# A new order of all steps, four half sums moved from VectorE to accumulating DMAs, and two copies moved to ScalarE

## The chip, the cores and the metric

The kernel runs on one core of a Trainium2 chip. A core has a TensorE for matmuls (PE; its weight loads are listed as PEld), a VectorE (DVE), a ScalarE (ACT), a GpSimd (POOL) and a SyncE (SP), and 16 DMA engines that move data between the chip's memory and the on-chip memory. The engines run side by side; each executes its own instructions in the order in which they were written, and semaphores make one wait for another. The metric is the device time of one execution in microseconds (us). Lower is better.

## The reference

The reference is a gated linear attention followed by a feed-forward layer with a rational activation. For each of 4 batches and 8 heads of 48 columns, over 768 positions:

```python
f = 1.0 / (1.0 + np.exp(-f_logit))
for t in range(S):
    state = f[:, :, t, :, None] * state + np.einsum('bhd,bhe->bhde', k[:, :, t], v[:, :, t])
    y[:, :, t] = np.einsum('bhd,bhde->bhe', q[:, :, t], state)
```

The result, reordered to 3072 rows of 384, goes through the layer:

```python
h = x @ w_in                      # 384 -> 2048
P = a[0] + a[1] * h + a[2] * h2 + a[3] * h3
Q = 1.0 + np.abs(b[0]) * np.abs(h) + np.abs(b[1]) * h2
g = P / (Q + 1e-06)
return g @ w_out                  # 2048 -> 384
```

Inputs and output are float32; the kernel computes in bfloat16 with float32 accumulation.

## The kernel before

The work is cut into 12 units of 256 positions: three stretches of time for each of four batches. A unit is an attention part, which hands its state to the next unit of the same batch, and a feed-forward part on 2048 hidden columns, which stand as 16 blocks of 128. There is no loop that sets the order. A text named ORDER lists 824 steps, one after another; the code walks through it and records each step's instructions. A step's name is followed by its unit, then by the heads' range or by the first and last block it covers (`0 8` is the first half of the 16, `8 16` the second, `0 16` all). `@0` to `@3` names one of four places in PSUM that the step's result takes, and `>x` makes the step begin only behind the step x. Every engine, and every DMA queue, executes its steps in the order in which they stand in this text.

The steps of a unit's attention part are these. `ld` loads gates, keys, queries (from SP's queue) and values (from POOL's queue, which also converts them). `ef` and `ls` turn the gates into logarithms on ACT. `cs` sums them over time on PE, and `A` takes the exponential of plus and minus these sums on ACT. `xa` multiplies queries and keys by that on DVE, `xg` does the same on POOL. `T` transposes both on PE, and `Te` copies the transposes out of PSUM (on ACT if an `s` follows, else on DVE). `sc` forms scores on PE, `mk` masks them on DVE. `vm` copies slices of the values on POOL. `yb` and `yi` form the output from scores and from the old state, `ye` scales it into the feed-forward layer's input (`s` on ACT, `v` on DVE). `kv` and `si` form the new state, `ae` and `st` decay it. `cm`, `cz`, `cu`, `ci`, `fa`, `fb` and `fr` prepare constants, and `dz` runs matmuls whose result nobody reads.

The feed-forward part is: `h`, 12 matmuls for four blocks of hidden columns; `hy`, the copy of these to bfloat16 (on ACT, or on DVE if a `v` follows); `sq` (h2, the square) and `ab` (z, the absolute value) on DVE. Then the logarithm of Q is taken on ACT. Its argument is the sum z + h2, which is made in one of three ways: by matmuls with the identity (`u`, then `ln` on ACT), by a DVE add (`zv`, then `lz`), or by a DMA that adds h2 onto z in memory (`zd`, then `lz`). `ex` on ACT turns this into 1/Q. The numerator is built on DVE: `p1` (a[3]h + a[2]), `pm` (times h2), `p2` (a[1]h + a[0], written over h), then the sum of the two, either by a DVE add (`tv`) or by a DMA that adds (`ta`); `gm` multiplies by 1/Q. Last come `o` (the second matmul, four blocks for one of two halves of the positions), `oe` (copy out of PSUM) and `so` (store).

The accumulating DMAs `zd` and `ta` are issued by POOL, between its `vm` copies, `xg` products and loads. Three buffers each hold h and the numerator over successive units, two hold h2 and z. In the lines that follow a number behind an underscore tells such buffers apart; it differs between the two kernels.

Of the kernel before, what the change touches and what calls it, by code (L numbers as in the profile page):

```python
# [24 lines left out]
ld 1 v; yb 0 2 4 @2; mk 0 0; wi 4 8; st 0 0; A 1 1; wi 0 4; yb 0 0 2; xa 1 1; yi 0 1; si 0 1; dz 3 @0; A 1 0
xa 1 0; dz 3; st 0 1; ye 0 0 1 v; ye 0 1 3 s; T 1 @1; Te 1 s; vm 1 1; fb; vm 1 0; ld 2 v; h 0 8 12 @2
hy 0 8 12 v; vm 2 1; sc 1 0 @0; ef 2; sc 1 1 @3; vm 2 0; mk 1 1; ha 0 12 16 @1; hb 0 12 16; ld 3 f >ye.0.0.1
ls 2; kv 1 @2; si 1 0; dz 1 @3; cs 2 @3; hy 0 12 16; ae 1; mk 1 0; ld 2 k; yb 1 2 4 @0; ab 0 8 12; ld 3 v
yb 1 0 2; st 1 0; A 2 1; yi 1 1; si 1 1; ld 4 v; sq 0 8 12; A 2 0; h 0 4 8 @1; ye 1 s; ef 3; h 1 12 16 @3
hy 0 4 8; ls 3; sq 0 12 16; p1 0 8 16; ab 0 12 16; st 1 1; hy 1 12 16; h 1 8 12 @0; hy 1 8 12; h 0 0 4 @2  # L30
pm 0 8 16; p2 0 8 16; cs 3 @3; ld 2 q; ab 0 4 8; sq 0 4 8; hy 0 0 4; ld 3 k; ld 3 q; u 0 12 16 @1; xa 2 1
sq 1 8 16; A 3 1; xa 2 0; sq 0 0 4; ln 0 12 16; ld 4 f; h 1 4 8 @2; A 3 0; hy 1 4 8; T 2 @0; u 0 8 12 @3
p1 0 0 8; ab 0 0 4; ab 1 8 16; Te 2 s; h 1 0 4 @1; ln 0 8 12; p2 0 0 8; sc 2 0 @2; xa 3 0; xg 3 1 0 2 >xa.3.0
hy 1 0 4; kv 2 @0; sc 2 1 @3; mk 2 0; u 1 12 16 @2; si 2 0; xg 3 1 2 4 >mk.2.0; ex 0 8 16; mk 2 1; p1 1 0 16
# [73 lines left out]
def kernel(  # L108
# [161 lines left out]
    def ef(n, a0=0, a1=HP):  # L270
        f = unit(n)["f"][:, 2 * a0:2 * a1].rearrange("p h i d -> p (h i d)")
        nc.scalar.activation(f, f, AF.Exp, scale=-1.0)  # L272
# [255 lines left out]
    def zd(n, m0, m1):  # L528
        s = unit(n)
        nc.gpsimd.dma_start(out=fl(s["z"], m0, m1), in_=fl(s["h2"], m0, m1), accum_op=ALU.add)  # L530
# [106 lines left out]
```

## Time and profile before

| what | value |
|---|---|
| time, median of 3 runs | 215.97 us (213.47 to 216.31) |
| span of the profiled execution, first to last instruction | 212.2 us |
| time of that profiled execution itself | not given with the results |
| accumulating DMAs, `gall<-hy` (`ta`) and `z<-h` (`zd`) | 18 and 15 |
| bytes moved by DMA, mean rate over the span | 41.10 MB, 194 GB/s |

In the profile an instruction is named by the line of the code, its engine, its operation and its tiles. A group of equal instructions has a count, the busy time in us, the mean duration of one in ns, and the time that the engine stood idle ahead of them with what ended it. `L564` is the DVE add `tv`, `L526` the DVE add `zv`, `L560` and `L530` are the DMAs `ta` and `zd`, `L495` is `hy`, `L338` and `L336` are `Te` on DVE and on ACT, `L441` and `L442` are `ye` on DVE and on ACT, `L534` is `lz`, `L460` is `h`, `L578` is `o`. A busy engine can still be the one that nobody waits for, so the stages and the waits are read beside the shares.

### The profile page before, as it was taken

To read this page: it belongs to the slowest core of one execution; us is meant where nothing else is said; L and a number is where in the kernel's file an instruction comes from. 1 tells how busy PE (TensorE), PEld (TensorE's weight loads), DVE (VectorE), ACT (ScalarE), POOL (GpSimd) and SP (SyncE) were. 2 spreads that over 40 slices of the span, in tenths; PEclk is the share of its full clock that TensorE was granted. 3 is DMA by queue.
4 is the path that set the end of the run, shared out by engine and by line. 5 is a ranking of instruction groups with operands and counts; after the bars stand their busy time and mean duration, and the time that the engine had idled before them with its cause. 6 is when DMAs were issued, how large, how long until landed. Compare 5 with 4: busy or idle time off the path is not lost.

```text
span 212.2 us, 7141 instructions
## 1 busy us (share of the span) xinstructions
PE 202.0 (95%) x3167; PEld 140.4 (66%) x3167; DVE 200.3 (94%) x210; ACT 193.2 (91%) x195; POOL 86.5 (41%) x106
## 2 busy tenths in 40 slices
PE   4999999989999999999999999999999989999993
PEld 1466677557776675677686686686686667676551
DVE  4786989999999999999999999999999999999991
ACT  3565699999999999899999999999999999999990
POOL 6151222661324793633136447397356143133100
PEclk9999999999999999999999999999999999999999
DMA  5999999999899999999299999599997996949924
GB/s 138 244 200 215 233 241 223 255 235 214 152 187 74 237 207 240 259 197 213 73 237 238 238 235 182 97 191 244 201 189 150 186 173 117 198 89 274 204 116 153
DMA packets 60623, 41.10 MB, mean 194 GB/s; under 512 B 51120, under 2 KB 54960, under 8 KB 60592
## 3 DMA queue, kind: packets, MB, share of 16 engines
q0 software_dynamic: 20944, 21.76, 63.5%
q1 hardware_dynamic: 39360, 18.68, 34.1%
q8 instruction: 25, 0.41, 0.8%
q10 hardware_dynamic: 288, 0.20, 0.3%
q14 instruction: 6, 0.05, 0.1%
HBM read 25.17 MB, written 4.72 MB: 141 GB/s over the span
## 4 chain that ended last, share of the span: by engine, by line
PE 18%; ACT 16%; DVE 14%; issue 5%; DMA 4%; ACTq 0%; POOLq 0%
PE op L578 12%; PE hp L460 5%; ACT hy L495 4%; ACT qi L538 4%; DMA z<-h 4%; ACT lq L534 3%; DVE h L500 3%; DVE scm L359 2%; DVE gall L568 2%; ACT qkT L336 1%; DVE gall L542 1%; ACT A L303 1%; DVE z L508 1%; DVE gall L556 1%; DVE gall L564 1%
## 5 line engine op out<-in xcount | busy, mean ns | idle before, releaser
L578 PE MATMUL op<-w_out_sb,gall 128*128 128x384 bf16 x384 | 69.0, 326 | 0.0
L460 PE MATMUL hp<-xT,w_in_sb 128*128 128x256 bf16 x564 | 67.6, 273 | 1.4 <-ACT xT L442 0.7
L460 PEld LDWEIGHTS <-w_in_sb 128*128 128x128 bf16 x564 | 54.3, 98 | 11.2 <-issue 1.5
L578 PEld LDWEIGHTS <-gall 128*128 128x128 bf16 x384 | 36.2, 98 | 22.7 <-DVE gall L568 0.5
L495 ACT CAST hy<-hp 128x1024 bf16<-128x1024 f32 x47 | 49.3, 1090 | 1.1 <-PE hp L489 1.0
L538 ACT ACTIVATE qi<-lq 128x4096 bf16<-128x4096 f32 (+2 forms) x18 | 45.6, 2539 | 0.0
L534 ACT ACTIVATE lq<-z 128x2048 f32<-128x2048 bf16 (+1 forms) x20 | 36.8, 1878 | 0.3 <-DMA z<-h 0.3
L560 POOL DMA_DIRECT2D gall<-hy x18 | 19.3, 1124 | 28.4 <-DVE gall L556 10.8
L359 DVE TENSOR_TENSOR scm<-sc,mask 128x1024 bf16<-128x1024 f32 x24 | 28.8, 1217 | 0.6 <-PE sc L351 0.6
L314 POOL TENSOR_TENSOR qkp<-kn,A 128x384 bf16<-128x384 f32 x17 | 17.0, 1002 | 29.8 <-ACT alast L447 7.4
L500 DVE TENSOR_TENSOR h<-hy 128x4096 bf16<-128x4096 bf16 (+2 forms) x19 | 28.3, 1500 | 0.2 <-ACT hy L495 0.2
L568 DVE TENSOR_TENSOR gall<-gall,qi 128x4096 bf16<-128x4096 bf16 (+2 forms) x17 | 28.2, 1668 | 0.2
L366 POOL COPY vmp<-vn 128x128 bf16<-128x128 bf16 x24 | 20.3, 919 | 19.7 <-DMA vn<-in_v_dram 18.4
L556 DVE TENSOR_TENSOR gall<-gall,h 128x4096 bf16<-128x4096 bf16 (+2 forms) x17 | 28.2, 1665 | 0.0
L530 POOL DMA_DIRECT2D z<-h x15 | 14.9, 1051 | 24.9 <-DVE h L500 7.2
L303 ACT ACTIVATE A<-cs 128x768 f32<-128x768 f32 (+1 forms) x26 | 19.7, 800 | 3.7 <-PE cs L287 2.9
L547 DVE TENSOR_SCALAR hy<-hy,a_sb 128x4096 bf16<-128x4096 bf16 (+1 forms) x14 | 16.7, 1192 | 0.0
L542 DVE TENSOR_SCALAR gall<-hy,a_sb 128x4096 bf16<-128x4096 bf16 (+1 forms) x14 | 16.6, 1187 | 0.0
L508 DVE TENSOR_SCALAR z<-hy 128x4096 uint16<-128x4096 uint16 (+2 forms) x19 | 16.1, 853 | 0.0
L272 ACT ACTIVATE fn<-fn 128x768 f32<-128x768 f32 (+1 forms) x13 | 10.8, 831 | 5.4 <-DMA fn<-in_f_logit_dram 5.4
L194 POOL DMA_DIRECT2D vn<-in_v_dram x12 | 12.9, 1079 | 6.8 <-issue 6.8
L326 PE MATMUL tp<-ident,qkp 128*128 128x128 bf16 x192 | 12.8, 219 | 0.2
(74 smaller groups left out, 266.7 us busy)
## 6 DMA issues: line engine op xcount, KB each, us to landing
gall<-hy POOLq DMA_DIRECT2D x16, 512.0 KB, 7.0
z<-h POOLq DMA_DIRECT2D x13, 512.0 KB, 7.8
fn<-in_f_logit_dram SPq DMA_DIRECT2D x11, 384.0 KB, 8.4
kn<-in_k_dram SPq DMA_DIRECT2D x11, 384.0 KB, 9.4
qn<-in_q_dram SPq DMA_DIRECT2D x11, 384.0 KB, 9.7
out_dram<-osb SPq DMA_DIRECT2D x11, 384.0 KB, 3.5
vn<-in_v_dram POOLq DMA_DIRECT2D x12, 192.0 KB, 7.2
w_in_sb<-in_moe_w_in_dram POOLq DMA_DIRECT2D x4, 384.0 KB, 7.8
```

The lines of the kernel that those rows point to most:

```text
L303: nc.scalar.activation(t, src, AF.Exp, scale=1.0 if x else -1.0)
L359: return nc.vector.tensor_mul(t, s["sc", g].rearrange("s r a i t -> s (r a) (i t)"), mb)
L366: nc.gpsimd.tensor_copy(s["vm"][:, :, :, 32 * x:32 * x + 16], src)
L460: nc.tensor.matmul(t[:, m - m0, :], w_in_sb[:, kk, m * P:(m + 1) * P], s["x"][:, kk].rearrange("p i j t -> p (i j t)"), start=(kk == 0), s ...
L495: (nc.scalar.copy if eng == "s" else nc.vector.tensor_copy)(fl(big(s, "hy", "hy", 3), m0, m1), fl(s["hp", m0], 0, m1 - m0))
L500: return nc.vector.tensor_mul(fl(big(s, "h2", "h2", 2), m0, m1), fl(s["hy"], m0, m1), fl(s["hy"], m0, m1))
L534: nc.scalar.activation(fl(lq, m0, m1), fl(s["z"], m0, m1), AF.Ln, scale=regs[2], bias=1.0 + 1e-6)
L538: nc.scalar.activation(fl(qi, m0, m1), fl(lq, m0, m1), AF.Exp, scale=-1.0)
L556: return nc.vector.tensor_mul(fl(s["g"], m0, m1), fl(s["g"], m0, m1), fl(s["h2"], m0, m1))
L560: nc.gpsimd.dma_start(out=fl(s["g"], m0, m1), in_=fl(s["hy"], m0, m1), accum_op=ALU.add)
L568: return nc.vector.tensor_mul(fl(s["g"], m0, m1), fl(s["g"], m0, m1), fl(qi, m0, m1))
L578: nc.tensor.matmul(s["op", j][:, j, 0:DM], s["g"][:, m, P * j:P * j + P], w_out_sb[:, m, :], start=(s["on", j] == 1), stop=(s["on", j] == KF))
```

## The change

The text ORDER is replaced. Both have 824 steps. Most are the same step at another place in the text or in another PSUM place; these nine are different steps:

| before | after |
|---|---|
| `tv 1 8 16`, `tv 2 8 16`, `tv 4 8 16` (DVE adds) | `ta 1 8 16`, `ta 2 8 16`, `ta 4 8 16` (DMAs) |
| `zv 2 8 16` (DVE add) | `zd 2 8 16` (DMA) |
| `zv 5 8 16` on DVE, `zd 5 0 8` by DMA | `zd 5 8 16` by DMA, `zv 5 0 8` on DVE |
| `Te 0 0 2` (DVE) | `Te 0 0 2 s` (ACT) |
| `hy 0 8 12 v` (DVE) | `hy 0 8 12` (ACT) |
| `ye 3 s` (ACT) | `ye 3 v` (DVE) |

The rest of the diff makes several step functions return their instruction, so that a `>` mark can name them:

```diff
 ORDER = """
-ld 0 f 2 4; cu 1; cz 0; ab_ b a; ld 0 f 0 2; cz 2; ld 0 k 0 2; cu 0; ld 0 k 2 4; ld 0 q 2 4; ci; cm; dz 9 @0
...
+ld 0 f 0 2; cz 2; cu 0; cz 1; cz 0; ab_ b a; ld 0 f 2 4; ab_ a s; ld 0 q 2 4; ld 0 k 2 4; ld 0 k 0 2; ld 1 f
...
     def zd(n, m0, m1):
         s = unit(n)
-        nc.gpsimd.dma_start(out=fl(s["z"], m0, m1), in_=fl(s["h2"], m0, m1), accum_op=ALU.add)
+        return nc.gpsimd.dma_start(out=fl(s["z"], m0, m1), in_=fl(s["h2"], m0, m1), accum_op=ALU.add)
...
     def ta(n, m0, m1):
         s = unit(n)
-        nc.gpsimd.dma_start(out=fl(s["g"], m0, m1), in_=fl(s["hy"], m0, m1), accum_op=ALU.add)
+        return nc.gpsimd.dma_start(out=fl(s["g"], m0, m1), in_=fl(s["hy"], m0, m1), accum_op=ALU.add)
```

The same `return` is added to `ef`, `A`, `ae`, `hy`, `ln`, `lz` and `ex`.

Three places show how instructions moved. The first is DVE in the first unit, from the first transpose copy `Te 0 2 4` (`qkT<-tp`) on; `scm` is a masked score, `state` the new state, `xT` the output of `ye`. Before:

```order
L338 COPY qkT<-tp 128x4x256
L314 TENSOR_TENSOR qkp_87<-qn,A 128x2x4x48
L359 TENSOR_TENSOR scm_281<-sc,mask 128x1024
L338 COPY qkT<-tp 128x4x256
L359 TENSOR_TENSOR scm_367<-sc,mask 128x1024
L451 TENSOR_TENSOR state_1_97<-sv,alast 128x384
L314 TENSOR_TENSOR qkp_88<-kn,A 128x2x8x48
L314 TENSOR_TENSOR qkp_88<-qn,A 128x2x8x48
L451 TENSOR_TENSOR state_0_96<-sv,alast 128x384
L441 TENSOR_SCALAR xT<-y,sig 128x2x2x64
```

After:

```order
L338 COPY qkT<-tp 128x4x256
L229 TENSOR_TENSOR mask<-Ui 128x64 x2
L229 TENSOR_TENSOR mask<-Us 128x64
L229 TENSOR_TENSOR mask<-Ui 128x64
L314 TENSOR_TENSOR qkp_87<-qn,A 128x2x4x48
L359 TENSOR_TENSOR scm_293<-sc,mask 128x1024
L359 TENSOR_TENSOR scm_336<-sc,mask 128x1024
L451 TENSOR_TENSOR state_1_97<-sv,alast 128x384
L314 TENSOR_TENSOR qkp_88<-qn,A 128x2x8x48
L314 TENSOR_TENSOR qkp_88<-kn,A 128x2x8x48
L441 TENSOR_SCALAR xT<-y,sig 128x2x2x64
L451 TENSOR_TENSOR state_0_96<-sv,alast 128x384
```

The mask is built here instead of in the first microseconds, the second transpose copy has left DVE, and `ye 0` stands ahead of the second state.

The second place is ACT in the first and second unit. Before, from `ef 1` to `ae 1`:

```order
L272 ACTIVATE fn<-fn 128x768
L447 ACTIVATE alast<-sv 128x8
L277 ACTIVATE lsp_93<-fn 128x8x2x48
L303 ACTIVATE A<-cs 128x2x384 x2
L442 ACTIVATE xT<-y 128x2x4x64
L336 COPY qkT<-tp 128x1024
L272 ACTIVATE fn<-fn 128x768
L277 ACTIVATE lsp_92<-fn 128x8x2x48
L495 CAST hy_471<-hp 128x1024
L447 ACTIVATE alast<-sv 128x8
```

After, from `ls 1` to `ae 1`:

```order
L277 ACTIVATE lsp_93<-fn 128x8x2x48
L336 COPY qkT<-tp 128x4x128
L303 ACTIVATE A<-cs 128x2x384 x2
L447 ACTIVATE alast<-sv 128x8
L266 TENSOR_LOAD sig x2
L442 ACTIVATE xT<-y 128x2x4x64
L336 COPY qkT<-tp 128x1024
L272 ACTIVATE fn<-fn 128x768
L495 CAST hy_521<-hp 128x1024
L277 ACTIVATE lsp_92<-fn 128x8x2x48
L495 CAST hy_521<-hp 128x1024
L447 ACTIVATE alast<-sv 128x8
```

The half transpose copy (`qkT<-tp 128x4x128`) and the first `hy` are new on ACT; the second `ls` (`lsp_92`) stands behind that `hy`.

The third place is POOL around the sums of units 1 and 2; `vmp` is a `vm` copy, `qkp` an `xg` product, `vn` a load of values. Before:

```order
L314 TENSOR_TENSOR qkp_88<-kn,A 128x2x4x48
L194 DMA vn<-in_v_dram 128x8x96 x2
L314 TENSOR_TENSOR qkp_88<-kn,A 128x2x4x48
L560 DMA gall_1333<-hy_1144 128x2048
L366 COPY vmp_94<-vn 128x8x16
L194 DMA vn<-in_v_dram 128x8x96
L366 COPY vmp_95<-vn 128x8x16
L530 DMA z_807<-h_760 128x2048
```

After:

```order
L206 DMA w_out_sb<-in_moe_w_out_dram 128x4x384 x2
L530 DMA z_669<-h_584 128x2048
L366 COPY vmp_95<-vn 128x8x16
L194 DMA vn<-in_v_dram 128x8x96
L366 COPY vmp_94<-vn 128x8x16 x2
L560 DMA gall_1048<-hy_731 128x2048
L314 TENSOR_TENSOR qkp_88<-kn,A 128x2x4x48 x2
L366 COPY vmp_95<-vn 128x8x16
L560 DMA gall_1458<-hy_1089 128x2048
```

`z_669` is the new `zd 2 8 16`, `gall_1048` the new `ta 1 8 16`; `gall_1458` is `ta 2 0 8`, which stood first of the sums before (`gall_1333`).

More of the change, by code (lines that the diff above doesn't have):

```diff
@@ L25 @@
[L25 to L34, printed above, removed]
@@ new lines @@
+hy 0 0 4; h 1 4 8 @0; u 0 12 16 @2; A 3 0; A 3 1; hy 1 4 8; T 2 @3; ld 3 k; ld 3 q; ld 4 f; ln 0 12 16; ld 6 f
+Te 2 s; u 0 8 12 @0; ln 0 8 12; sq 1 8 16; h 1 0 4 @2; sc 2 0 @3; kv 2 @0; ld 4 k; ld 4 q; hy 1 0 4; sq 0 0 4
+vm 2 0; ex 0 8 16; p1 0 0 8; ab 1 8 16; ab 0 0 4; ab 0 4 8; ld 5 f; xa 3 0; pm 0 0 8; ld 3 v; vm 2 1; ld 5 v
+wo 8 12; wo 12 16; xg 3 1 0 2 >xa.3.0; si 2 0; sc 2 1 @1; u 1 12 16 @2; ae 2; ln 1 12 16; mk 2 0
+xg 3 1 2 4 >mk.2.0; mk 2 1; st 2 0; u 0 4 8 @3; u 0 0 4 @1; yb 2 2 4 @2; ef 4; yi 2 1; yb 2 0 2; ln 0 0 4; ye 2 s
@@ new lines @@
+ld 8 f; ld 6 q; ld 7 k; xg 5 1 2 4 >pm.2.0.16; yb 4 2 4; yb 4 0 2; cs 6 @0; o 0 0 8 12; lz 2 8 16; ye 4 s; ld 6 k
+u 2 0 4 @1; st 4 1; ab 3 0 16; sq 3 0 16; p1 3 0 16; gm 1 8 16; gm 1 0 8; A 6 0; oe 0 0 2 s; ln 2 0 4; A 6 1
+h 4 4 8 @3; T 5 @2; h 4 12 16 @1; ef 7; h 4 0 4 @0; hy 4 4 8; Te 5 s; hy 4 12 16; ex 2 8 16; hy 4 0 4; sc 5 0 @2
+h 4 8 12 @3; mk 5 0; o 1 1 8 12 @1; zv 3 8 16; u 2 4 8 @2; o 1 1 4 8; hy 4 8 12; sc 5 1 @0; kv 5 @3; p2 3 0 16
+xa 6 0; ln 2 4 8; mk 5 1; vm 5 1; ta 2 0 8; ld 6 v; ta 2 8 16; zd 3 0 8; xg 6 1 2 4 >mk.5.0; ae 5
@@ new lines @@
+xg 6 1 0 2 >gm.1.8.16; ls 7; o 1 0 8 12; o 1 0 4 8; si 5 0; o 1 1 0 4; cs 7 @2; st 5 0; ex 2 0 8; ef 8; si 5 1
+yb 5 2 4 @0; yb 5 0 2; A 7 0; sq 4 0 16; yi 5 1; yi 5 0; A 7 1; st 5 1; ld 8 q; o 1 0 12 16; ld 11 f; ld 9 k
+ld 9 q; ld 8 k; ye 5 s; o 1 1 12 16; T 6 @3; h 5 4 8 @0; lz 3 8 16; pm 3 0 16; ab 4 0 16; gm 2 0 16; Te 6 s
+o 1 0 0 4; kv 6 @2; ld 8 v; vm 6 1; zd 4 0 8; hy 5 4 8; ta 3 0 8; oe 1 0 2 s; si 6 0; xg 7 1 0 2 >gm.2.0.16
+ta 3 8 16; h 5 8 12 @3; sc 6 1 @0; h 5 0 4 @1; ls 8; ae 6; hy 5 8 12; lz 3 0 8; hy 5 0 4; o 2 1 12 16 @3
@@ new lines @@
+o 2 1 4 8; o 2 0 0 4; o 2 0 12 16; sc 6 0 @1; p1 4 0 16; st 6 0; mk 6 1; p2 4 0 16; xa 7 0; ex 3 0 16; zd 4 8 16
+vm 6 0; vm 7 1; xg 7 1 2 4 >st.6.0; mk 6 0; o 2 0 8 12; h 5 12 16 @0; si 6 1; pm 4 0 16; hy 5 12 16; o 2 0 4 8
+T 7 @1; o 2 1 0 4; lz 4 0 8; yi 6 0 @0; yi 6 1; ab 5 0 16; Te 7 s; st 6 1; yb 6 2 4; yb 6 0 2; o 2 1 8 12
+cs 8 @2; sc 7 1 @1; ye 6 s; h 6 0 4 @0; oe 2 0 2 s; A 8 1; A 8 0; hy 6 0 4; ef 11; sq 5 0 16; h 6 4 8 @3
+hy 6 4 8; mk 7 1; h 6 12 16 @2; sc 7 0 @0; kv 7 @1; p1 5 0 16; gm 3 0 16; hy 6 12 16; si 7 0; o 3 0 0 4 @3
@@ new lines @@
+so 3 0 2 s; hy 7 8 12; ld 11 q; ld 10 k; ld 10 q; Te 8; hy 7 0 4; kv 8 @2; p1 6 0 16; xa 9 0; si 8 0
+o 4 0 4 8 @1; ls 10; lz 5 0 8; ae 8; sc 8 1 @3; zd 6 8 16; sc 8 0 @0; lz 6 8 16; zd 6 0 8; vm 8 0; ta 5 0 8
+ld 10 v; o 4 0 12 16; o 4 1 0 4; o 4 0 0 4; xg 9 1 0 2 >gm.4.0.16; xg 9 1 2 4 >p1.6.0.16; mk 8 0; mk 8 1
+h 7 12 16 @0; yb 8 0 2 @3; hy 7 12 16; o 4 1 8 12; o 4 0 8 12; o 4 1 4 8; st 8 0; pm 6 0 16; yi 8 0; yi 8 1
+yb 8 2 4; p2 6 0 16; ab 7 0 16; sq 7 0 16; ex 5 0 16; kv 9 @2; si 9 0; o 4 1 12 16; cs 10 @0; ye 8 s; oe 4 0 2 s
@@ new lines @@
+o 7 0 0 4; o 7 1 4 8; hy 11 12 16; ex 9 0 16; o 8 1 0 4 @2; h 11 8 12 @3; o 8 1 4 8; o 8 0 4 8; h 11 0 4 @1
+o 8 0 0 4; o 8 0 8 12; o 8 1 8 12; sq 10 0 16; o 8 0 12 16; o 8 1 12 16; ab 10 0 16; hy 11 8 12; zv 10 0 8
+p1 10 0 16; ta 9 8 16; ta 9 0 8; ab 11 12 16; pm 10 0 16; p2 10 0 16; gm 9 0 16; lz 10 0 8; sq 11 12 16
+sq 11 8 12; p1 11 8 16; zd 10 8 16; ab 11 8 12; lz 10 8 16; o 9 1 0 4 @3; oe 7 0 2 s; so 5 0 2 s; so 6 0 2 s
+ex 10 0 16; o 9 1 8 12; o 9 1 12 16; ta 10 0 8; pm 11 8 12; o 9 0 8 12; h 11 4 8 @0; tv 10 8 16; o 9 0 12 16
@@ new lines @@
+o 9 0 0 4; o 9 1 4 8; o 9 0 4 8; p2 11 8 16; zd 11 12 16; gm 10 0 16; hy 11 0 4; hy 11 4 8; lz 11 12 16
+pm 11 12 16; sq 11 0 4; sq 11 4 8; ab 11 0 4; ab 11 4 8; p1 11 0 8; zd 11 8 12; lz 11 8 12; oe 8 0 2 s
+ex 11 8 12; oe 9 0 2 s; ex 11 12 16; ta 11 8 12; so 9 0 2 s; o 10 1 12 16 @0; o 10 0 8 12; o 10 0 12 16
+so 8 0 2 s; so 7 0 2 s; zv 11 0 4; p2 11 0 8; o 10 0 0 4; u 11 4 8 @2; o 10 1 0 4; gm 11 8 12; ta 11 12 16
+ln 11 4 8; ex 11 4 8; lz 11 0 4; o 10 1 8 12; o 10 0 4 8; o 11 1 8 12 @3; o 10 1 4 8; pm 11 4 8; gm 11 12 16
@@ L99 @@
+tv 11 4 8; ex 11 0 4; oe 10 0 2 s; gm 11 4 8; pm 11 0 4; tv 11 0 4; o 11 1 12 16; o 11 0 12 16 @1; o 11 1 4 8
+o 11 0 4 8; o 11 0 8 12; gm 11 0 4; so 10 0 2 s; o 11 0 0 4; o 11 1 0 4; oe 11 1 2 s; oe 11 0 1 v; dz 1 @1
+so 11 0 1 s; so 11 1 2 a
 """
@@ L271, in ef @@
         f = unit(n)["f"][:, 2 * a0:2 * a1].rearrange("p h i d -> p (h i d)")
-        nc.scalar.activation(f, f, AF.Exp, scale=-1.0)
+        return nc.scalar.activation(f, f, AF.Exp, scale=-1.0)
     def ls(n, a0=0, a1=HP):
@@ L494, in hy @@
         s = unit(n)
-        (nc.scalar.copy if eng == "s" else nc.vector.tensor_copy)(
+        return (nc.scalar.copy if eng == "s" else nc.vector.tensor_copy)(
             fl(big(s, "hy", "hy", 3), m0, m1), fl(s["hp", m0], 0, m1 - m0))
```

118 lines of the change are left out of this document (45 added, 73 removed).

## Prediction

> **What bounds the kernel now.** I read the page's busy line, then a table by stages, then who waits for whom, then the chain of waits from its end. The page:
>
> ```profile
> span 212.2 us, 7141 instructions
> PE 202.0 (95%) x3167; PEld 140.4 (66%) x3167; DVE 200.3 (94%) x210; ACT 193.2 (91%) x195; POOL 86.5 (41%) x106
> ```
>
> Three engines are nearly full, so the averages decide nothing. The stage table has for each stretch the busy time of PE, PEld, DVE, ACT and POOL, then clock, share of the DMA engines and GB/s:
>
> ```profile
> 0.00:27.00 27.00, 23.18 (x419) 14.53 (x420) 20.59 (x53) 14.70 (x24) 8.98 (x23) 1.00 1.14 206
> 27.00:171.00 144.00, 140.99 (x2437) 101.13 (x2434) 143.41 (x121) 142.71 (x145) 69.74 (x75) 1.00 1.04 199
> 171.00:208.60 37.60, 37.55 (x321) 24.70 (x313) 35.78 (x37) 35.81 (x29) 7.74 (x10) 1.00 0.76 173
> 208.60:212.20 3.60, 0.32 (x2) 0.00 (x0) 0.56 (x1) 0.00 (x0) 0.00 (x0) 1.00 0.32 114
> ```
>
> In the head (0 to 27) ACT idles 12.3 of 27 us and DVE 6.4. In the middle both are full at once: DVE lacks 0.6 us of 144, ACT 1.3 us. In the tail PE is full. ACT's waits for the whole span name those gaps:
>
> ```profile
> ACT fn L272 <- DMA fn<-in_f_logit_dram: 5.4, 4, 2.3
> ACT A L303 <- PE cs L287: 2.9, 3, 1.2
> ACT xT L442 <- DVE xT L441: 2.1, 1, 2.1
> ...
> ACT A L303 <- DVE qkp L314: 0.8, 1, 0.8
> ACT lq L534 <- DMA z<-h: 0.3, 1, 0.3
> ACT alast L447 <- PE sv L431: 0.2, 1, 0.2
> ```
>
> The last three are the whole 1.3 us of the middle; a DMA's sum was late once, by 0.3 us. The chain at its end runs on PE without a break:
>
> ```profile
> 171.14 1.47 PE hp L460 x12
> ...
> 191.42 8.52 PE op L578 x52
> 199.94 0.86 PE u L516 x4
> 200.80 7.83 PE op L578 x48
> ...
> 208.66 0.56 DVE osb L585
> ```
>
> **The change, part by part.** Times of a step are taken from its start to the next start, since neighbours overlap a little.
>
> Half sums off DVE. DVE loses `tv 1 8 16`, `tv 2 8 16`, `tv 4 8 16` and `zv 2 8 16`; in unit 5 it only swaps its half.
>
> ```profile
> 91.30 1.14 DVE gall L564
> ...
> 110.21 1.13 DVE z L526
> ```
>
> Four at 1.13 to 1.14 us are 4.5 us off DVE.
>
> The copies. `Te 0 0 2` and `hy 0 8 12` leave DVE for ACT, and `ye 3`, which the change's title doesn't name, comes from ACT to DVE. The DVE timeline, then ACT's:
>
> ```profile
> 11.94 0.68 DVE L338 COPY qkT<-tp 128x1024 bf16<-128x1024 bf16 x1
> ...
> 16.98 0.48 DVE L441 TENSOR_SCALAR xT<-y,sig 128x256 bf16<-128x256 f32 x1
> 17.37 0.74 DVE L260 TENSOR_SCALAR a_sb<-a_sb,sig 128x3 f32<-128x3 f32 x3
> 19.72 1.23 DVE L495 CAST hy<-hp 128x1024 bf16<-128x1024 f32 x1 [1.61 <-PE hp L460]
> ```
>
> ```profile
> 55.10 0.85 ACT L442 ACTIVATE xT<-y 128x768 bf16<-128x768 f32 x1
> 55.80 1.07 ACT L521 ACTIVATE lq<-u 128x1024 f32<-128x1024 f32 x1
> ...
> 144.16 1.99 ACT L495 CAST hy<-hp 128x1024 bf16<-128x1024 f32 x2
> 145.96 3.71 ACT L538 ACTIVATE qi<-lq 128x4096 bf16<-128x4096 f32 x1
> ```
>
> DVE: minus 0.7 and minus 1.2. `ye 3` is three times the 256 columns that took 0.39 us; my estimate is 0.9, between 0.39 and 1.17, nearer the upper end because most of the time grows with columns. DVE in all: -4.5 - 0.7 - 1.2 + 0.9 = -5.5 us. ACT: plus 0.9 for `hy 0 8 12` (two casts in 1.80 us) and about 0.5 for half a transpose copy (half of that), both in the head; minus 0.7 for `ye 3` (55.10 to 55.80), in the full middle. ACT in all: +0.7 us. So the stretch from 27 to 171 has 0.7 us less ACT work, and DVE gets some 4 us of room there that ACT can't follow.
>
> The waits in ACT's middle. The 0.8 us wait for a DVE product should go, since DVE gets ahead; the 0.3 us wait for the sum of unit 6 too, since its operands are ready earlier. I count -1.1 and leave the 0.2. What is late next there is nothing that the profile shows: ACT simply has 142 us of work. Bounds: 0 to -1.3.
>
> The head. Here the order is new on every engine. The first `sc` now waits behind `kv 0`, and the mask is built between `Te 0 2 4` and `xa 0 0 0 2`, so the first masked scores come about 1 us later; unit 1's gates are loaded one place earlier, and `ef 1` and `ls 1` move up. Both copies moved to ACT fall into its 12.3 idle us, but `ls 2`, then `cs 2` and `A 2`, stand behind `hy 0 8 12`. Against that DVE no longer has the half copy (0.7) ahead of the second masked scores, and `ye 0` overtakes `st 0 1`. Followed through step by step, `ye 1` comes out 0 to 0.5 us later, ahead of a wait of ACT that hides part of it:
>
> ```profile
> 26.83 0.84 ACT L272 ACTIVATE fn<-fn 128x768 f32<-128x768 f32 x1 [0.97 <-DMA fn<-in_f_logit_dram]
> ```
>
> Unit 3's gates are asked for behind `ye 0`, as before. Loss at most 1.4 us (both copies on the path), gain at most 3.1 (the 2.1 us wait for `ye 0` and this 1.0 us both gone). I take +0.3, nearer the loss, because nothing on the path gets shorter. PE's warm-up matmuls are 27 as before: nothing.
>
> The four added sums on DMA. DMA rows, then stages:
>
> ```profile
> q0 software_dynamic: 20944, 21.76, 63.5%
> q1 hardware_dynamic: 39360, 18.68, 34.1%
> ```
>
> ```profile
> gall<-hy POOLq DMA_DIRECT2D x16, 512.0 KB, 7.0
> z<-h POOLq DMA_DIRECT2D x13, 512.0 KB, 7.8
> ```
>
> ```profile
> 27.00:60.00 33.00, 31.10 (x512) 22.50 (x510) 32.41 (x36) 32.94 (x40) 12.35 (x16) 1.00 1.19 220
> 60.00:120.00 60.00, 59.74 (x1020) 42.09 (x1019) 60.00 (x49) 59.04 (x60) 28.92 (x28) 1.00 1.00 199
> ```
>
> ```profile
> L560 POOL DMA_DIRECT2D gall<-hy x18 | 19.3, 1124 | 28.4 <-DVE gall L556 10.8
> L530 POOL DMA_DIRECT2D z<-h x15 | 14.9, 1051 | 24.9 <-DVE h L500 7.2
> ```
>
> POOL issues four more at 1.1 us: 4.4 us on an engine busy 41%. Each takes 7 to 8 us to land where DVE took 1.1, so the question is the slack. The tightest is `zd 2 8 16`:
>
> ```profile
> 58.47 2.29 DVE L500 TENSOR_TENSOR h<-hy 128x4096 bf16<-128x4096 bf16 x1
> ...
> 69.51 1.92 ACT L534 ACTIVATE lq<-z 128x2048 f32<-128x2048 bf16 x1
> ```
>
> The squares are written at 60.7, plus 7.8 is 68.5, and ACT asks at 69.5 less 0.7: 0.3 us of slack. Behind it in POOL's queue stand `vm 5 0`, the load of unit 7's values, both `vm 4` and then `ta 1 8 16`:
>
> ```profile
> L366 POOL COPY vmp<-vn 128x128 bf16<-128x128 bf16 x24 | 20.3, 919 | 19.7 <-DMA vn<-in_v_dram 18.4
> ```
>
> ```profile
> 79.07 2.44 DVE L568 TENSOR_TENSOR gall<-gall,qi 128x2048 bf16<-128x2048 bf16 x2
> ```
>
> From 60.7 two issues (2.2) and three copies (2.8) lead to 65.7 for `ta 1 8 16`, which lands at 72.7. Its reader is `gm 1`, which started at 79.07 and now has `tv 1` (1.1) and `pm 3` (2.2) no longer ahead of it: 75.8, so 3 us of slack. `ta 2` and `ta 4` stand 8 us and more ahead of their readers. Bounds: 0 (33 such sums cost 0.3 us so far) to 3 us (one landing late by half its time, on ACT). I take +0.5, nearer the rows.
>
> [...]
>
> The tail. Behind `yi 11` PE has in both orders 7 `h` blocks, 40 `o` blocks, one `u` and two `yb`: 0.
>
> Sum: -0.7 - 1.1 + 0.3 + 0.5 = -1.0 us on a span of 212.2. The results give no time for the profiled execution itself; the median of the three runs, 215.97, is 3.8 us above its span. I leave those 3.8 us as they are: 215.0 us.
>
> **The rivals.**
>
> DVE is the limit. The full 5.5 us come off: 215.97 - 5.5 = 210.5 us. For it: DVE is fuller than ACT, by 0.7 us in the middle. Against: ACT has 1.3 us of room there. It decides only if ACT's head shortens as well, by 3 us or more. [...]
>
> The DMA engines are the limit: the other sign. q0 and q1 together fill 97.6% of the span. Four sums are 2.1 MB on top of some 11.9 MB (199 GB/s for 60 us) in the stage from 60 to 120, where all four are due. If the 220 GB/s of the stage before is the ceiling, 14.0 MB take 63.8 us: +3.8. By q0's own rate (134.7 us for 21.76 MB) they take 13 us. Half of that on the path, less the 1.0 gained, gives about +6: 222 us. It decides from the point at which loads or sums land more than 3 us later than now. Against: the share passes 1.00 in three of the stages shown, so packets overlap and 97.6% isn't a ceiling, and ACT waited 0.3 us in all for sums. [...]
>
> A new wait in order of issue: `zd 2 8 16` or unit 2's gates late by 3 us on ACT, or the head late by 1.4 and more. About +2: 218 us.
>
> **Numbers.** Mine 0.58, DVE 0.14, DMA 0.16, new wait 0.12. The likeliest alone: 213 to 217. The range takes in the new wait, most of the DVE rival and the lower half of the DMA rival: 211 to 220. About 2% (4.3 us) is what a measurement of this kernel can tell from no change. Faster by more: DVE 0.14 and 0.01 of mine, 0.15. Slower by more: DMA 0.16 and 0.01 of the new wait, 0.17. Within: 0.68.
>
> **What would show it.** Right: in the middle stage DVE falls to some 138 of 144 us with waits on ACT, ACT stays above 142; `ye 1` ends 0 to 0.5 us later than before; PE still runs unbroken from about 170 to the end; no ACT wait for a sum over 1 us. Wrong: ACT waiting several us on `z<-h` or on gate loads, sums landing at 10 us and more (DMA); ACT's idle head under 9 us (then faster than I say); a gap on PE behind 171.

## The result, and the profile after

| | before | after |
|---|---|---|
| median of the runs | 215.14 us (213.47 to 216.31) | 222.97 us (222.66 to 224.64) |
| ratio after to before | | 1.0403, 95% interval 1.0353 to 1.0453 |
| span of the profiled execution | 212.2 us | 221.1 us |
| time of the profiled execution | not given | 222.76 us |

The kernel became 4% slower; the prediction had 215.0 us and a range from 211 to 220. Executions more than 1.5% above the fastest of the same kernel are left out of the ratios and, in the experiments, of the medians. From the page of the changed kernel, the span, the busy time of each engine, the granted clock in 40 slices, the two DMA queues, and the rows of the products `xg` on POOL and `xa` on DVE (busy us, mean ns of one):

```profile
span 221.1 us, 7149 instructions
PE 201.8 (91%) x3167; PEld 140.8 (64%) x3167; DVE 205.2 (93%) x205; ACT 195.6 (89%) x196; POOL 96.8 (44%) x110
PEclk9999889999999999999999999999999999999999
q0 software_dynamic: 21520, 23.86, 67.2%
q1 hardware_dynamic: 39360, 18.68, 33.1%
L314 POOL TENSOR_TENSOR qkp<-kn,A 128x384 bf16<-128x384 f32 x17 | 27.0, 1592 | 21.1 <-DVE scm L359 6.7
L314 DVE TENSOR_TENSOR qkp<-qn,A 128x768 bf16<-128x768 f32 (+1 forms) x13 | 16.8, 1293 | 2.5 <-DMA qn<-in_q_dram 2.5
```

The row of `xg` on the page of the kernel before:

```profile
L314 POOL TENSOR_TENSOR qkp<-kn,A 128x384 bf16<-128x384 f32 x17 | 17.0, 1002 | 29.8 <-ACT alast L447 7.4
```

DVE lost four adds and two copies and yet is busy for 4.9 us more (200.3 to 205.2). And the 17 `xg`, the same instructions as before, take 1592 ns each in place of 1002. Head and middle of the changed kernel, columns as in the prediction:

```profile
0.00:27.00 27.00, 20.23 (x383) 12.25 (x384) 16.57 (x46) 14.35 (x23) 9.37 (x23) 0.99 1.08 196
27.00:171.00 144.00, 135.08 (x2374) 97.97 (x2360) 143.52 (x117) 136.55 (x139) 75.45 (x74) 0.99 1.09 206
```

In the middle DVE is still full (143.52 of 144), while ACT has fallen from 142.71 to 136.55 and PE from 140.99 to 135.08: DVE is now the only engine that is full there. In the head DVE idles 10.4 us (27 less 16.57) where it idled 6.4. So the 8.9 us by which the span grew are, on DVE, 4.0 us more idle time, all of it in the head, and 4.9 us more busy time.

Where DVE's busy time comes from is seen in the timeline of DVE, then of POOL, at one place (start, duration):

```profile
131.82 1.86 DVE L542 TENSOR_SCALAR gall<-hy,a_sb 128x4096 bf16<-128x4096 bf16 x1
133.60 2.71 DVE L314 TENSOR_TENSOR qkp<-qn,A 128x768 bf16<-128x768 f32 x1
136.24 1.21 DVE L359 TENSOR_TENSOR scm<-sc,mask 128x1024 bf16<-128x1024 f32 x1
...
132.33 3.17 POOL L314 TENSOR_TENSOR qkp<-kn,A 128x384 bf16<-128x384 f32 x2
```

`p1 6` takes 1.86 us where it took 1.34, `xa 9 0` 2.71 where it took 0.95, and the two `xg` lie beside them. In the kernel before an `xg` pair stood beside the mask products `mk`, whose operand comes from PSUM:

```profile
157.63 2.35 DVE L359 TENSOR_TENSOR scm<-sc,mask 128x1024 bf16<-128x1024 f32 x2
...
157.86 2.07 POOL L314 TENSOR_TENSOR qkp<-kn,A 128x384 bf16<-128x384 f32 x2 [2.22 <-ACT qkT L336]
```

Neither is longer there than elsewhere in that kernel: its 17 `xg` take 0.995 to 1.024 us each, and a `mk` at 131.85 us, while POOL is idle, takes 1.13 us to the next start, these two 2.27. Each DVE step of the changed kernel was set against the same kind of step's usual duration: twelve steps that overlap an `xg` are longer by 9.2 us together, all lengthened steps by about 10.9. In the kernel before that sum is about 1.0. The 5.5 us that the prediction takes off DVE and these 9.9 us more make +4.4, near the 4.9 measured. The marks did not change: of the seventeen `xg` sixteen begin behind the same step as before, and the last one's `zv 5 8 16` became `zd 5 8 16`. But the DVE steps that follow the marked ones are others. By the step that each `xg` overlaps longest, 16 of the 17 lie beside a `mk` in the kernel before, and 3 in the changed one.

### The profile page after: what moved, and what is told of

The parts are those of the page before. It is cut to its first block, busy times and chain, and to the rows that moved or that the text cites. A ratio compares the mean times of both kernels' runs of the same rounds, so it can differ in the third digit from the quotient of the medians.

```text
span 221.1 us, 7149 instructions
## 1 busy us (share of the span) xinstructions
PE 201.8 (91%) x3167; PEld 140.8 (64%) x3167; DVE 205.2 (93%) x205; ACT 195.6 (89%) x196; POOL 96.8 (44%) x110
## 4 chain that ended last, share of the span: by engine, by line
DVE 59%; issue 11%; PE 9%; ACT 9%; DMA 8%; SPq 2%; DVEq 0%
DVE scm L359 9%; DVE gall L568 8%; DVE gall L556 8%; DVE h L500 8%; DVE qkp L314 5%; DVE gall L542 5%; PE op L578 5%; DVE hy L547 5%; DVE z L508 5%; DMA fn<-in_f_logit_dram 4%; DMA qn<-in_q_dram 4%; DVE state L451 4%; ACT qi L538 3%; PE hp L460 3%; ACT hy L495 2%
## 5 line engine op out<-in xcount | busy, mean ns | idle before, releaser
L460 PE MATMUL hp<-xT,w_in_sb 128*128 128x256 bf16 x564 | 68.7, 275 | 3.6 <-DVE scm L359 2.3
L314 POOL TENSOR_TENSOR qkp<-kn,A 128x384 bf16<-128x384 f32 x17 | 27.0, 1592 | 21.1 <-DVE scm L359 6.7
L534 ACT ACTIVATE lq<-z 128x2048 f32<-128x2048 bf16 (+1 forms) x20 | 35.5, 1812 | 0.0
L560 POOL DMA_DIRECT2D gall<-hy x21 | 22.1, 1082 | 29.1 <-DVE hy L547 17.8
L530 POOL DMA_DIRECT2D z<-h x16 | 17.7, 1133 | 24.2 <-DVE h L500 7.8
L303 ACT ACTIVATE A<-cs 128x768 f32<-128x768 f32 (+1 forms) x26 | 18.8, 780 | 0.8 <-PE cs L287 0.6
L314 DVE TENSOR_TENSOR qkp<-qn,A 128x768 bf16<-128x768 f32 (+1 forms) x13 | 16.8, 1293 | 2.5 <-DMA qn<-in_q_dram 2.5
L547 DVE TENSOR_SCALAR hy<-hy,a_sb 128x4096 bf16<-128x4096 bf16 (+1 forms) x14 | 18.2, 1301 | 0.0
L542 DVE TENSOR_SCALAR gall<-hy,a_sb 128x4096 bf16<-128x4096 bf16 (+1 forms) x14 | 17.6, 1258 | 0.0
L508 DVE TENSOR_SCALAR z<-hy 128x4096 uint16<-128x4096 uint16 (+2 forms) x19 | 17.4, 927 | 0.0
## 6 DMA issues: line engine op xcount, KB each, us to landing
qn<-in_q_dram SPq DMA_DIRECT2D x11, 384.0 KB, 11.4
```

Source lines behind the costliest of these rows:

```text
L314: return eng.tensor_mul(s["qk"][:, :, x, hh, 0:D], s["qk"[x]][:, hh].rearrange("p h i d -> p i h d"), A_sb[:, :, x].rearrange("p i (h d) - ...
L460: nc.tensor.matmul(t[:, m - m0, :], w_in_sb[:, kk, m * P:(m + 1) * P], s["x"][:, kk].rearrange("p i j t -> p (i j t)"), start=(kk == 0), s ...
L534: return nc.scalar.activation(fl(lq, m0, m1), fl(s["z"], m0, m1), AF.Ln, scale=regs[2], bias=1.0 + 1e-6)
L542: return nc.vector.tensor_scalar(fl(big(s, "g", "gall", 3), m0, m1), fl(s["hy"], m0, m1), a_sb[:, 3:4], a_sb[:, 2:3], op0=ALU.mult, op1=AL ...
L547: i = (nc.gpsimd if eng == "p" else nc.vector).tensor_scalar(fl(s["hy"], m0, m1), fl(s["hy"], m0, m1), a_sb[:, 1:2], a_sb[:, 0:1], op0=ALU ...
```

## The experiments

Each ratio is to the kernel before, run on the same chip, with its 95% interval. The diffs in this part show pieces of ORDER's lines and leave out steps that did not move. A collision is, from here on, a product on POOL and a DVE step that hold each other up.

| run | median us | ratio |
|---|---|---|
| a1_xg_beside_mk | 217.63 | 1.0172 (1.0144 to 1.0199) |
| b1_xg_off_mk | 231.01 | 1.0756 (1.0688 to 1.0823) |
| c1_products_added | 230.85 | 1.0755 (1.0670 to 1.0839) |
| c2_products_twelve | 220.91 | 1.0299 (1.0240 to 1.0358) |
| c3_writes_twelve | 214.71 | 1.0010 (0.9968 to 1.0053) |
| a3_coefs_later | 220.69 | 1.0318 (1.0286 to 1.0351) |
| a9_scaling_only | 223.44 | 1.0409 (1.0335 to 1.0482) |
| b3_copies_on_act | 215.94 | 1.0049 (1.0018 to 1.0079) |
| a4_both | 215.41 | 1.0000 (0.9966 to 1.0035) |
| a5_three_more | 216.30 | 1.0065 (1.0027 to 1.0103) |
| a2_sums_on_dve | 230.05 | none; 4 runs, 228.89 to 237.51 us |
| b2_sums_on_dma | 218.74 | 1.0164 (1.0082 to 1.0247) |
| b4_copies_on_dve | 221.01 | 1.0337 (1.0212 to 1.0462) |
| a7_less_act | 215.60 | 1.0061 (1.0023 to 1.0098) |
| a8_less_dve | 216.44 | unclear; 4 runs, 215.13 to 221.67 us |
| a10_less_both | 215.88 | 1.0064 (1.0024 to 1.0105) |
| a11_less_both_loads_up | 214.91 | 0.9998 (0.9968 to 1.0029) |
| a12_both_loads_up | 215.34 | 1.0023 (0.9995 to 1.0051) |

### Products on POOL beside DVE

a1 gives most `xg` of the changed kernel a place beside `mk`, for instance:

```diff
-xg 9 1 0 2 >gm.4.0.16; xg 9 1 2 4 >p1.6.0.16; mk 8 0; mk 8 1
+xg 9 1 0 2 >xa.9.0; mk 8 0; xg 9 1 2 4 >mk.8.0; mk 8 1
```

> The changed kernel, with thirteen of the seventeen products that POOL computes (xg, L314) given other places: each begins beside a mask product of DVE (mk), as in the kernel before, instead of beside xa, p1, p2 or ab. Nothing else changes. Theory P (a product on POOL and certain DVE instructions hold each other up): in the changed kernel the DVE instructions that overlap an xg are 9.2 us longer in all than the same steps elsewhere, and the xg take 27.1 us for 17 where they took 17.0. With the xg beside mk I expect xg at about 1.0 to 1.2 us each, DVE's stretch under 2.5 us, and the time 5 to 8 us lower, 215 to 218 us. Theory D (the DMA engines are the limit, as the prediction's second rival had it): the DMA work is the same, so the time stays within 1.5 us of 223, whatever becomes of xg.

It came to 217.63 us, 5.3 less and in the range expected. In its profile the row of `xg`, then DVE and POOL at the place shown above:

```profile
L314 POOL TENSOR_TENSOR qkp<-kn,A 128x384 bf16<-128x384 f32 x17 | 17.8, 1051 | 20.0 <-ACT A L303 4.8
```

```profile
129.13 0.94 DVE L314 TENSOR_TENSOR qkp<-qn,A 128x768 bf16<-128x768 f32 x1
129.99 2.34 DVE L359 TENSOR_TENSOR scm<-sc,mask 128x1024 bf16<-128x1024 f32 x2
...
130.16 2.13 POOL L314 TENSOR_TENSOR qkp<-kn,A 128x384 bf16<-128x384 f32 x2 [2.00 <-DVE qkp L314]
```

`xa 9 0` is back at 0.94 us. DVE's lengthened steps fell from 10.9 to 4.0 us, the span from 221.1 to 214.3: 6.9 and 6.8. (This profiled execution is a1's fastest; the medians differ by 5.3.)

b1 does the reverse in the kernel before (units 6 to 10):

```diff
-xg 6 1 0 2 >gm.1.8.16; mk 5 0; xg 6 1 2 4 >mk.5.0; mk 5 1; st 5 0
+mk 5 0; mk 5 1; st 5 0; xg 6 1 0 2 >st.5.0; xg 6 1 2 4 >st.5.0
```

> The kernel before, with ten xg (units 6 to 10) begun one or two DVE steps later, so that they run beside p1, p2, xa and tv and not beside mk. No step changes its engine and DVE's order stays. Theory P: each pair of xg costs DVE 0.9 to 2.3 us, as such pairs did in the changed kernel; DVE is full in the middle, so the time rises by 4 to 8 us, to 219 to 223 us, and xg goes from 1.0 to about 1.6 us. Theory D, or that xg is slow only because POOL's queue is crowded in the changed kernel: no more than 1 us, 214 to 216 us.

231 us is far over what was expected. Its DVE steps are longer by 5.0 us beside the `xg`, as the theory has it; much of the rest comes with the edit itself, since later products are waited for (PE 4.7 us for `qkp`) and hold up the copies `vm` behind them in POOL's queue (PE 5.9 us for these). So this run shows the collision but not its price. c1 and c2 add products that nobody waits for to the kernel before:

```diff
+    def xd(mark):
+        m = _at(mask, [[0, 2], [1, DM // 2]])
+        behind(nc.gpsimd.tensor_mul(scr, m, m), mark[1:])
```

> The kernel before, with thirteen more products on POOL of the size of an xg (128x384 to bf16, read from the mask, written to a tile that nobody reads), each begun so that it runs beside DVE steps between tiles in SBUF (p1, p2, ab, sq, xa, zv, tv, gm) while POOL is idle; all else as before. They add nothing that any engine waits for. Theory P, with the price seen so far (0.7 to 0.8 us for each product that meets such a step): 13 x 0.75 = about 10 us more on DVE, which lacks 0.6 us of being full in the middle, so the time rises by 6 to 10 us, to 221 to 225. If POOL's products cost DVE nothing by themselves, and the changed kernel's stretched steps had another cause: 214 to 216.

> The kernel before with twelve added products on POOL, those of the run with thirteen without the last, which had waited 9 us for a gap and made a sum late. In that run these twelve lengthened DVE's steps by 0.42 to 0.64 us each, 6.9 us in all. Theory P: DVE is full, so the time rises by 5 to 8 us, to 219 to 222. If most of the 16.7 us there were the one late sum and its consequences: below 217.

c1, at 230.85 us, also comes out over its range (221 to 225), for a reason that its timeline shows: its last product took 9.15 us, a sum behind it in POOL's queue was late, and ACT stood 7 us for it:

```profile
168.51 9.15 POOL L322 TENSOR_TENSOR scr<-mask 128x384 bf16<-128x384 f32 x1 [0.20 <-DVE scm L364]
...
182.32 1.91 ACT L539 ACTIVATE lq<-z 128x2048 f32<-128x2048 bf16 x1 [7.04 <-DMA z<-h]
```

c2, without that product, comes to 220.91 us, in the range expected: its twelve products lengthen DVE's steps by 0.47 to 0.64 us each, 6.9 in all, and the span grows by 6.9 (219.1 against 212.2). Two of them meet the DVE steps `pm 4` (not shown), `p2 4` and `gm 3`:

```profile
104.04 1.84 DVE L552 TENSOR_SCALAR hy<-hy,a_sb 128x4096 bf16<-128x4096 bf16 x1
105.81 2.91 DVE L573 TENSOR_TENSOR gall<-gall,qi 128x4096 bf16<-128x4096 bf16 x1
...
102.07 4.51 POOL L322 TENSOR_TENSOR scr<-mask 128x384 bf16<-128x384 f32 x2 [0.20 <-DVE scm L364]
```

By these times the first product starts inside `pm 4`, waits for its end, then runs and keeps `p2 4` waiting (1.84 us for 1.33), and the second does the same with `p2 4` and `gm 3` (2.91 for 2.28). c3 has writes at the same places:

```diff
-        m = _at(mask, [[0, 2], [1, DM // 2]])
-        behind(nc.gpsimd.tensor_mul(scr, m, m), mark[1:])
+        behind(nc.gpsimd.memset(scr, 1.0), mark[1:])
```

> As the run with twelve added products, with a write of a constant to the same tile in place of each product (128x384 to bf16, nothing read). If what collides is the reading on POOL, the steps with two operands in SBUF (sq, tv, gm, xa) keep their 2.28, 1.21, 2.28 and 0.95 us, and the time is within 2 us of before, 213 to 216. If any work of POOL on that memory collides, or if a crowded POOL queue is what costs, the time is that of the twelve products.

214.71 us, no difference to before. DVE (`pm 4`, `p2 4`, `gm 3`), then POOL:

```profile
99.50 2.27 DVE L560 TENSOR_TENSOR gall<-gall,h 128x4096 bf16<-128x4096 bf16 x1
101.70 1.33 DVE L551 TENSOR_SCALAR hy<-hy,a_sb 128x4096 bf16<-128x4096 bf16 x1
102.96 2.27 DVE L572 TENSOR_TENSOR gall<-gall,qi 128x4096 bf16<-128x4096 bf16 x1
...
99.69 0.42 POOL L321 MEMSET scr<- 128x384 bf16 x1 [0.17 <-DVE scm L363]
101.89 1.50 POOL L321 MEMSET scr<- 128x384 bf16 x1 [1.78 <-DVE gall L560]
```

Beside the two-operand step `pm 4` the write runs at once (0.42 us); beside `p2 4` it waits for the end (1.50); DVE loses nothing (2.27, 1.33 and 2.27 us for the three steps, 200.3 us busy in all, as before). So in these two runs DVE's steps, the two-operand `gm 3` among them, are longer beside a product, which reads on POOL (2.91 us), and not beside a write, which reads nothing (2.27). The DMAs are the same in both; POOL is also less crowded here (9.6 us for the twelve writes, 25.3 for the twelve products), but no DVE step is longer beside a write. Why the write waits at `p2` and not at `pm` is not shown. The 9.15 us product of c1 lasted through more than one step: it began while a `pm` ran, and let three more two-operand steps (`xa` 0.94 us, `sq` 2.28, `gm` 2.28) and one `ab` (1.21) of DVE pass that began after it, one behind the other without a gap.

### The head

a3 puts the small load of the coefficients and their scaling `fb` back to where the kernel before has them:

```diff
-ld 0 f 2 4; ab_ a s; ld 0 q 2 4
+ld 0 f 2 4; ld 0 q 2 4
...
-ld 0 v; ef 0 0 2
+ld 0 v; ab_ a s; ef 0 0 2
...
-cz 3; fb
+cz 3
```

> The changed kernel, with two things of its head as in the kernel before: the load of the four coefficients into all partitions (2 KB in 16-byte packets) is asked for behind the load of unit 1's gates and no longer ahead of unit 0's queries and keys, and the scaling of the coefficients stands behind the first part of ye 0. In the changed kernel's trace the DMA engines move 12 GB/s in the slice in which those packets come (4.5 to 5.3 us), where the kernel before has 281 to 306, and the first product of DVE waits 1.9 us for the queries. Theory H1 (these packets hold up the loads behind them): that hole goes, unit 0's queries land 1.0 to 1.5 us earlier, and with DVE full from 29 us on the time falls by 0.8 to 1.5 us, to 221.3 to 222. Theory H2 (the head's 2.8 us come from the order on PE and DVE alone): within 0.5 us of 223.

220.69 us, 2.3 less, more than expected. Windows of 0.5 us of the kernel before, of the changed one and of a3 (last columns: clock, DMA share, GB/s):

```profile
4.50:5.00 0.50, 0.50 (x3) 0.16 (x2) 0.42 (x4) 0.42 (x1) 0.00 (x0) 1.00 1.13 297
5.00:5.50 0.50, 0.50 (x2) 0.15 (x1) 0.41 (x4) 0.40 (x1) 0.00 (x0) 1.00 1.18 321
```

```profile
4.50:5.00 0.50, 0.50 (x3) 0.15 (x1) 0.43 (x4) 0.40 (x2) 0.00 (x0) 1.00 0.76 12
5.00:5.50 0.50, 0.50 (x2) 0.15 (x1) 0.43 (x4) 0.50 (x2) 0.00 (x0) 1.00 0.29 20
```

```profile
4.50:5.00 0.50, 0.50 (x3) 0.15 (x1) 0.43 (x4) 0.46 (x1) 0.00 (x0) 1.00 1.20 280
5.00:5.50 0.50, 0.50 (x2) 0.15 (x1) 0.43 (x5) 0.35 (x2) 0.00 (x0) 1.00 1.51 187
```

While the 16-byte packets of a 2 KB load stand ahead of 960 KB of others, the 16 engines move 12 to 20 GB/s. `ab_ a s` in the diff is that load. a9 moves the scaling alone:

> The changed kernel, with the scaling of the coefficients on DVE put behind ye 0 as in the kernel before, while their small load stays ahead of unit 0's queries and keys. Theory H1 (the 16-byte packets hold up the loads behind them): the hole at 4.5 us stays and the time is within 0.7 us of 223.0. If the scaling's place on DVE was what cost: 220.7, as with both moved.

223.44 us, no gain, and the engines still move only 12 and 25 GB/s in these two windows. a3 differs from a9 by the load's place alone, so that is the cause. b3 makes only the three small moves between DVE and ACT, in the kernel before (`Te 0 0 2 s`, `hy 0 8 12`, `ye 3 v`):

> The kernel before, with only the three small moves between DVE and ACT (half the copy of unit 0's transposes and the first cast of hy to ACT, the scaling of unit 3 to DVE). The prediction put the head at +0.3 and unit 3 at -0.7: within 1 us of before, 213.1 to 215.1. If the copies on ACT are what makes the head late, 1.5 us higher or more.

215.94 us, 0.5% (0.2 to 0.8) over before: a small loss where the prediction had a small gain, and not the head's loss.

### Both repairs

a4 is a1 and a3 together; a5 takes out three more collisions.

> The changed kernel with both repairs at once: the xg beside the mask products of DVE, and the load and scaling of the coefficients later in the head. Alone, the one gave 217.6 us and the other 220.7, where the changed kernel has 223.0. If collisions and head are two independent losses, 217.6 - 2.3 = 215.3 us, within 1 us of that and of the kernel before. If DVE were the limit as the prediction's first rival had it, its 5.5 us of relief would now come out: 210 to 212 us. In the run with the xg moved ACT has no gap over 1.1 us from 24 us to the end, so I take the first.

> As the kernel with both repairs, with three collisions more taken out (half of unit 4's keys multiplied on DVE; the xg of units 6 and 8 begun elsewhere), worth some 1.7 us of DVE time by the run with the xg moved. If DVE is still what the end waits for, 1 to 1.7 us less than that kernel; if ACT is, less than 0.7.

a4 comes to 215.41 us, as expected from two independent losses: 5.3 and 2.3 alone, 7.6 together. By the ratios it is 2.3 and 0.9% alone and 4.0% together, so that they are independent is known to about 1% only. With both repairs the change is worth nothing: ratio 1.0000, 0.9966 to 1.0035. Its head and middle:

```profile
0.00:27.00 27.00, 21.35 (x403) 12.98 (x404) 17.36 (x48) 15.32 (x25) 9.19 (x23) 1.00 1.11 203
27.00:171.00 144.00, 139.34 (x2402) 101.51 (x2408) 142.70 (x120) 141.48 (x142) 75.51 (x77) 1.00 1.12 215
```

The head is not as it was: DVE idles 9.6 of these 27 us (6.4 before, 10.4 in the changed kernel), and `ye 1` begins at 26.7 us (25.0 and 27.8). Against that DVE is busy 2.4 us less than before in all (197.9 against 200.3). So in this trace a4 still has a later head and some collisions (lengthened steps 3.75 us against 1.0 before), and part of DVE's relief is spent on them.

a5 is 0.65% over before. It took three collisions out and brought others (lengthened steps 4.5 us against a4's 3.75): moving a product by hand moves it beside the next step.

### What the relief of DVE is worth

Put back on DVE in the changed kernel, the four sums cost more than their 4.5 us; taken off it in the kernel before (`tv 1 8 16` to `ta 1 8 16` and so on, each asked for early), they gain nothing; and with four copies of transposes moved from ACT to DVE on top of that, it gets slower:

> The changed kernel, with the four half sums that it gave to DMAs put back on DVE, in the same places of the order. Theory D: four transfers of 512 KB fewer, so the time falls by 3 us or more, under 220 us. Theory P with DVE as the limit from 29 us on: DVE gets 4 x 1.13 = 4.5 us more work, POOL four issues less (which may also shift an xg), so the time rises by 3 to 5 us, to 226 to 228 us.

> The kernel before, with only the four half sums given to DMAs (each asked for 7 us or more ahead of its reader), and no other step moved: DVE gets 4.5 us less work, and the DMAs 2.1 MB more. The prediction's main step (ACT has 142 us of work in 144 and can't follow): 0 to 1.5 us lower, 212.6 to 214.3 beside a before of 214.1. DVE as the limit: 4 us lower, about 210. The DMA engines as the limit: 3 us or more higher, above 217.

> The kernel before with the four half sums on DMA, as in the run with that alone (218.7 us), and four copies of transposes (units 5, 7, 9 and 10, 1.05 us each on ACT, some 0.7 to 1.2 on DVE) moved from ACT to DVE, where that run left 9 us idle in the middle. If ACT's amount of work sets the time there: 3 to 4 us lower, about 215. If the order of steps with its waits between the engines does, and not the amount: within 1.5 us of 218.7.

230.1, 218.7 and 221.0 us. a2 contradicts the DMA theory in sign; its DVE is busy only 3.8 us more than the changed kernel's (209.0 against 205.2), and where the rest of its 7 us comes from is open. b2 lies where the DMA theory put it, but is inconclusive as a price: in its profiled execution 3.3 of the 5.6 us more are there at 52.8 us, before POOL issues the first of the moved sums at 58.8. PE had stood in the midst of a group of matmuls, and the twelve matmuls behind that took 2.72 us in place of 1.47, at a granted clock of 0.50 from 50 to 52 us and 0.60 from 52 to 53:

```profile
49.61 0.30 PE L420 MATMUL sv<-vn,qkp 64*64 64x48 bf16 x6 [2.14 <-issue]
49.84 0.38 PE L426 MATMUL sv<-ind,lsp 128*128 128x2 bf16 x8
50.08 2.72 PE L460 MATMUL hp<-xT,w_in_sb 128*128 128x256 bf16 x12
```

Behind that DVE waits 2.0 us for queries (at 90.2 us) and PE 1.0 us for values (at 116.7 us), which the kernel before doesn't, so some price of the added DMAs isn't ruled out in b2. It does show that DVE's room isn't followed: DVE idles 9 us in its middle. Nor did b4 follow; why it is slower is open. Then work was left out of a4: a7 omits half of the exponentials of units 4 and 6 (ACT), a8 half of `gm` of units 4, 6 and 7 (DVE), a10 both.

> The kernel with both repairs, with the second half of two of ACT's exponentials left out (units 4 and 6, 1.8 us each; these halves of the reciprocal keep the unit before's values): ACT has 3.7 us less to do, DVE as much as ever. If ACT is what the middle waits for once the collisions are gone, as the prediction had it: 2 to 3.7 us lower than 215.4. If DVE is: within 1 us of it.

> The kernel with both repairs, with half of three of DVE's last products left out (gm of units 4, 6 and 7, 1.15 us each; these halves are not multiplied by the reciprocal): DVE has 3.4 us less to do, ACT as much as ever. If DVE is what the middle waits for: 2 to 3.4 us lower than 215.4. If ACT is: within 1 us of it.

> The kernel with both repairs, with less work on ACT and on DVE at once (the halves of two exponentials, 3.7 us, and of three products, 3.4 us, that the two runs before left out one after the other; what is not computed keeps old values). If ACT and DVE are both full in the middle, so that relief of one is worth nothing, relief of both is: 212 to 213.5, some 2 to 3.5 us under 215.4. If a third thing (DMAs, PE, the order's waits) sets the time: within 1 us of 215.4.

None gains by the ratios or, for a8, by its median; a8's four runs spread from 215.1 to 221.7, which its trace (213.4 us of span) doesn't explain, so for DVE alone the evidence is thin. In a10 a wait has come that a4 doesn't have, DVE's of 2.7 us for unit 10's queries; SP had asked for them behind a store that stood until unit 3's output was there (SPq is SP's queue):

```profile
141.71 0.96 DVE L314 TENSOR_TENSOR qkp<-qn,A 128x768 bf16<-128x768 f32 x1 [2.70 <-DMA qn<-in_q_dram]
```

```profile
106.87 16.44 SPq L591 DMA_DIRECT2D out_dram<-osb  x2
...
125.65 5.70 SPq L194 DMA_DIRECT2D qn<-in_q_dram  x1
```

a11 and a12 put those loads ahead of the store, in a10 and in a4:

```diff
-so 2 0 2 s
+so 2 0 2 s; ld 11 q; ld 10 k; ld 10 q
...
-so 3 0 2 s; hy 7 8 12; ld 11 q; ld 10 k; ld 10 q
+so 3 0 2 s; hy 7 8 12
```

> The kernel with both repairs and less work on ACT and DVE (as the run before it: halves of two exponentials and of three products left out), with three loads of SP's queue (unit 11's queries, unit 10's keys and queries) ahead of the store of unit 3's output and no longer behind it. If that load is the third limit, its 2.7 us of wait on DVE go: the span falls from 214.1 by 2 us or more, to about 212, and the time to 213.5 or less. If the waits of the order as such are the limit, another takes its place: less than 1 us.

> The kernel with both repairs and all its work, with the same three loads moved up. DVE waits there for no load of unit 10, since it is busy until the load has come; so the time stays within 0.7 us of 215.4. If the late loads slow something that the trace does not name, 1 us or more lower, which would be under the kernel before.

In a11 the wait is gone and the span falls from 214.1 to 212.2, but with 7 us of work left out the time is still that of before (0.9998) and not the 213.5 us or less that was expected; a12 changes nothing, as expected. No version beat the kernel before.

## Why the prediction was wrong

- **"DVE in all: -5.5 us"** is the step that failed. It priced the steps that change their engine and put the cost of the seventeen `xg`, which stay on POOL but get other neighbours on DVE, at nothing without a reason. Beside `mk` they cost nothing; beside `xa`, `p1`, `p2` and `ab` (and 0.3 us beside one `pm`) they cost DVE 9.2 us. DVE's busy time rose by 4.9. That this is the cause is shown by a1 (5.3 us of the 7.8 come back), c2 and c3.
- **"The head ... +0.3"** failed too. It followed the scores, the gates and the copies, and passed over the 2 KB load that moved ahead of the queries and keys; "loss at most 1.4" was no bound. That load cost 2.3 us (a3, a9). `ye 1` came 2.8 us later in the changed kernel, not 0 to 0.5; with the load back in its place it is still 0.6 us later in a3's trace and 1.7 in a4's, which stays unexplained.
- **"DVE gets some 4 us of room there that ACT can't follow"** was near in what it said of the time, under conditions that the changed kernel doesn't meet: with the two repairs it runs 215.4 us, where the prediction had 215.0. That is partly luck, since a4 still has a later head and some collisions. The reason given, "ACT simply has 142 us of work", is not shown: less work on ACT gains nothing either (a7), nor less on both. DVE, ACT and PE all stand within 5 us of full in a4's middle, in a fixed order; that what one of them gains the next takes is argued and not shown. Which hand-over holds the time when ACT and DVE both have less to do stayed open beyond the one load that a11 names.
- **The sums on DMA** (+0.5): right that they are hidden, and even less than allowed for. ACT waited for no sum at all, and sums land in 6.3 and 6.8 us (7.8 and 7.0 before). So the DMA rival fails by its own condition, loads or sums more than 3 us later, though the time it gave, 222, is near: the largest shift of a median is that of the queries, 9.7 to 11.4 us, and a2, with fewer DMAs, is slower; only b2's waits for loads speak for it. ACT's waits in the changed kernel, of which those for gates (`fn`) all lie in the head:

```profile
ACT fn L272 <- DMA fn<-in_f_logit_dram: 7.9, 3, 3.7
...
ACT hy L495 <- PE hp L460: 5.4, 8, 2.2
```

- **`ye 3` on DVE**: 0.9 estimated, 0.92 measured from its start to the next start (59.15 to 60.07 us). **The tail**: right, PE is busy for 46.5 of the 47 us from 171 us on.
- **The rivals**: "a new wait in order of issue", with "the head late by 1.4 and more", named one of the two losses and its size (+2), though not its cause, and nothing named the other.
